# Pooled attention, then four attention experts: two batches' first output with tokens on the rows, turned by the DMA crossbar

## The chip, the core and the metric

The kernel runs on one core of a Trainium2 chip. The core has a matrix engine (PE, with a separate row for its weight loads, PEld), a vector engine (DVE), a scalar engine (ACT), a general engine (POOL) and a queue for transfers (SP). Data live in SBUF, 128 partitions; PE writes only to PSUM, which has eight banks of 512 fp32 columns in each partition, and DVE and ACT read it from there. The metric is the device time of one execution in microseconds (us); lower is better.

## What is computed

Eight batches of 576 tokens with eight heads of 64. Keys and values are averaged over groups of 8 tokens (72 pooled keys), each token attends to them, and the output, heads side by side, is the input x (576 x 512) of a mixture of four causal attention experts, of which each token takes the two with the largest gate.

```python
k_p = k.reshape(B, H, Sp, pool, D).mean(axis=3)
v_p = v.reshape(B, H, Sp, pool, D).mean(axis=3)
attn = softmax(scale * np.matmul(q, k_p.transpose(0, 1, 3, 2)))
x = np.matmul(attn, v_p).transpose(0, 2, 1, 3).reshape(B, S, H * D)
...
for e in range(E):
    q, k, v = x @ wq[e], x @ wk[e], x @ wv[e]
    a = softmax(causal(scale * (q @ k.transpose(0, 2, 1))))
    ye = a @ v @ wo[e]
    out += (gate weight of expert e) * ye
```

## The kernel before

The program is one long list of steps, the string SEQ, written out by a planner. Each token of it names a step, its arguments, its batch, the PSUM bank or banks it uses, and, with a trailing d, that a copy goes to DVE and not to ACT. The list is walked once; every engine gets its own instructions in that order and works them off strictly in that order. So the list sets the order of work on PE, ACT, DVE, POOL and SP, and the PSUM banks. Capital letters are PE's steps, small letters what reads their banks.

The steps of one batch b, with the lines that the profile shows:

- L loads q, k and v, converted to bf16 on the way, on POOL's queue (L124). Three buffers of each kind are used in turn.
- PK, PV pool keys and values on PE (L205, as most matmuls); kc, kt and vc bring the results to SBUF (kpT; vp, 96 pooled rows by 8 heads by 64). u turns q by 32 x 32 blocks on DVE (L281).
- E, e: scores of the 8 heads, pooled keys on the rows, tokens in the columns; ACT takes the exponential (L314) into eta.
- D, d, x: the sum over the pooled keys, by matmuls of eta with a constant matrix (onesd), for 4 heads at a time, each in a strip of 32 rows; ACT takes its logarithm (d, L333) and then exp of its negative (x, L337), which leaves the reciprocal in rza.
- O, o: vp times eta, again in four strips of 32 rows, so that a head's features lie on the rows and the tokens in the columns; DVE multiplies by rza (o, L360 for the 512 main tokens, L351 for the last 64) into xT, which is x turned, features on the rows.
- P, p: xT times the experts' query and key weights; p copies to qk. V, v: xT as weights, times the experts' value and gate weights; v copies values (vaug) and gate logits. g: the gates, ten small steps.
- S, s: causal score blocks; s is the exponential on ACT (L477, L471), a the causal mask on POOL (L494, L486).
- B, bz, bg, b: scores times values with a column of ones that gives the sum; reciprocal, gate factor and multiplication on DVE (L529, L531, L536) into osc, tokens on the rows.
- T, t turn osc on PE and copy it into oT (L214, L196); in batches 2 to 5, F does that by the DMA crossbar from SP's queue instead (L561 for the last 64 tokens, L564 for the 512 others).
- Y, y, z: oT times the output weights, the copy to ofin (L196) and the store (L599, L595 for the last 64 tokens of two batches), from SP's queue.

Batches go in pairs: batches 2n and 2n + 1 share one xT, in which the last 64 tokens of both lie in one block of 128 columns. Before, xT is laid out as 128 partitions x 4 feature groups x 1152 columns. The steps of neighbouring batches are interleaved, so that while ACT takes exponentials of one batch, PE works on another. A wait arises where a step of one engine needs a result, or a bank, of another that is not there yet; all later steps of that engine stand behind it. At the start, H steps are matmuls on zeros that fill PE's idle time.

Of the kernel before, what the change touches and what calls it, by code (L numbers as in the profile page):

```python
# [21 lines left out]
def kernel(  # L22
# [33 lines left out]
    KR = 96  # L56
# [70 lines left out]
    def plain(c):  # L127
        return xTs[1][0:KR].rearrange("p f n -> p (f n)").bitcast(FP32)[:, 512 * c : 512 * c + 512]
# [94 lines left out]
    def mcols(b):  # L223
        return slice(640 * (b % 2), 640 * (b % 2) + MAIN)

    def tcols(b):
        return slice(MAIN + 64 * (b % 2), MAIN + 64 * (b % 2) + TAIL)


# [41 lines left out]
    def vc(b, bank, dve):  # L271
        copy(dve, vps[b % 2][:], psum[0:KR, bank, :].rearrange("j (h d) -> j h d", d=D))
# [67 lines left out]
    def Ov(b, bank, g, t):  # L340
        got = pieces(b, g)
        for j, cols, o in got:
            for u in range(2) if g == 2 else [t]:
                for i, h, eta in heads(b, j, cols):
                    at_ = o * 2 + TAIL * u if g == 2 else o
                    mm(psum[32 * i : 32 * i + 32, bank, at_ : at_ + eta.shape[1]], vps[b % 2][:, h, u::2], eta)

    def ov(b, bank, dve, g, t):
        xT, rz = xt(b), part(rzas[b % 2], b, g)
        if g == 2:  # L350
            nc.vector.tensor_tensor(  # L351
                out=xT[:, :, tcols(b)].rearrange("p (g t) n -> p g t n", t=2),
# [4 lines left out]
        else:  # L357
            got = pieces(b, g)
            m = mcols(b).start
            nc.vector.tensor_tensor(  # L360
                out=xT[:, 2 * got[0][0] + t : 2 * got[-1][0] + t + 1 : 2, m + got[0][1].start : m + got[0][1].stop],
                in0=psum[:, bank, :].rearrange("p (g n) -> p g n", g=len(got)), in1=rz, op=MULT,
            )
# [69 lines left out]
    def P(b, bank, nm, ep):  # L433
        jobs = [(m, e) for m in "qk" for e in range(NEP)] if nm == "t" else [(nm, ep)]
        cols, n = (tcols(b), TAIL) if nm == "t" else (mcols(b), MAIN)
# [122 lines left out]
    def crossbar(b, ep, tail):  # L558
        oT, own = oTs[2 * (b // 2 % 2) + ep], osc(b, ep)
        if tail:  # L560
            nc.sync.dma_start(out=oT[:, tcols(b)], in_=own[half(b), 4 * (1 - b % 2), :], transpose=True)  # L561
        else:
            c = b % 2
            nc.sync.dma_start(out=oT[:, mcols(b)].rearrange("p (c n) -> p c n", n=128), in_=own[:, c : c + 4, :].rearrange("p c n -> p (c n)"), transpose=True)  # L564
# [26 lines left out]
    def z(b, c, queue):  # L591
# [9 lines left out]
    MATRIX = {"PK": PK, "PV": PV, "E": Es, "D": Dn, "O": Ov, "V": V, "P": P,  # L601
# [7 lines left out]
        H1:0@0 W1:0 PK1:0@0 L_k0:1 E0:0@24 kc1:0 H1:0@1 L_k1:1 kt1:0d H1:0@1 e00:0 H1:0@0 H1:0@0 H1:0@0 u1:0 L_k2:1  # L609
        e01:0 L_q0:1 E2:0@02 E1:0@46 e20:0 e21:0 L_q1:1 e11:0 D2:0@2 D0:0@3 d0:0 PV:0@0 L_q2:1 e10:0 H1:0@1 H1:0@1  # L610
        vc:0d H1:0@1 H1:0@1 x0:0 O01:0@3 c0:0d L_q3:1 O10:0@4 d2:0 D1:0@5 o01:0 x2:0 O00:0@0 O20:0@2 d1:0 O11:0@1 o00:0
        H1:0@6 H1:0@3 x1:0 H1:0@3 W2:0 c2:0d H1:0@3 c1:0d H1:0@0 H1:0@0 o10:0 H1:0@0 H1:0@0 W3:0 o11:0 H1:0@0 H1:0@0
        o20:0 P_q0:0@3 c3:0d L_v0:1 P_k0:0@2 p_q0:0 L_v1:1 P_t0:0@1 p_k0:0 L_v2:1 PK:1@3 p_t0:0 S00:0@4 L_k0:2 kc:1
        S03:0@0 S01:0@6 P_k1:0@2 s03:0 kt:1d s01:0 L_k1:2 P_q1:0@3 u1:1 L_k2:2 p_k1:0 s00:0 u0:1 a01:0 E1:1@06 a03:0
        p_q1:0d L_q0:2 e10:1 c4:0d E2:1@24 L_q1:2 e20:1 e21:1 L_q2:2 E0:1@02 e11:1 V2:0@4 a00:0 L_q3:2 e00:1 V3:0@5
        v2:0d V1:0@6 v3:0d e01:1 V0:0@4 L_v0:2 v1:0d D0:1@5 v0:0d D2:1@7 PV:1@0 d0:1 g1:0 D1:1@6 L_v1:2 H1:0@1 g0:0
        vc:1d x0:1 H1:0@1 H1:0@1 g2:0 d1:1 O01:1@0 L_v2:2 g3:0 O11:1@1 d2:1 O00:1@5 o01:1 x2:1 O20:1@6 O10:1@7 x1:1
        S02:0@2 o00:1 W4:0 H1:0@4 s02:0 o11:1 S10:0@4 L_k0:3 o20:1 S11:0@0 s10:0 o10:1 S12:0@2 L_k1:3 PK:2@6 g4:0 s11:0
        V2:1@7 L_k2:3 kc:2 P_t0:1@4 s12:0 kt:2d V0:1@6 L_q0:3 P_q0:1@5 u0:2 a02:0 p_t0:1 v0:1 u1:2 v2:1 E0:2@02 L_q1:3
        p_q0:1 g5:0 B01:0@4 g6:0 e00:2 L_q2:3 g7:0 P_k0:1@5 g8:0 g9:0 a10:0 bz01:0 e01:2 bg01:0 E1:2@06 L_q3:3 b01:0  # L620
        p_k0:1d B00:0@4 a11:0 e10:2 V3:1@2 L_v0:3 bz00:0 bg00:0 B10:0@5 b00:0 PV:2@3 e11:2 a12:0 bz10:0 v3:1d D0:2@4
        P_k1:1@0 vc:2d L_v1:3 d0:2 bg10:0 b10:0 E2:2@26 x0:2 L_v2:3 O00:2@4 p_k1:1d e21:2 D1:2@5 O01:2@1 e20:2 o00:2
        O10:2@6 L_k0:4 d1:2 O11:2@0 o01:2 PK:3@7 x1:2 L_k1:4 S01:1@2 kc:3 S02:1@4 P_q1:1@1 s01:1 o10:2 L_k2:4 o11:2
        s02:1 V4:1@7 L_q0:4 T01:0@6 p_q1:1d S00:1@2 t01:0 L_q1:4 v4:1d S03:1@4 s00:1 S11:1@0 P_q1:2@6 u1:3 a02:1 s03:1
# [129 lines left out]
```

## Time and profile before

| | us |
|---|---|
| median of three runs | 157.75 |
| lowest and highest | 156.88, 159.96 |
| the profiled execution, own time | 156.05 |
| its span, first to last instruction | 154.3 |

The time of an execution holds a little more than the span. The busy shares of the engines, the table of windows and the groups by line are shown in the prediction, each where it is used. A group's row reads: line, engine, operation, written tile <- read tiles, partitions x elements and type, count | busy us in total, mean ns of one | idle us of the engine before them, and what ended it. A row of the timeline reads: start us, length us, engine, line, operation, count of merged instructions.

The inputs are loaded throughout the first part: the last of POOL's load instructions starts at 85.1 us, and the first crossbar transfer of SP's queue at 91.8 us.

### The profile page before, as it was taken

Reading aid. Unit: us, or ns where it says so; the run is one execution under the profiler, and the core shown is the slowest. Engines: PE = TensorE matmul, PEld = TensorE weight load, DVE = VectorE, ACT = ScalarE, POOL = GpSimd, SP = SyncE. Lnnn points to the kernel's source line nnn. Section 1 sums busy time; section 2 is a strip of 40 time slices with the busy share of each in tenths; the row PEclk is TensorE's granted clock in tenths of the full one; section 3 lists DMA queues with packets and bytes.
Section 4 is the critical chain, followed back from the end, with each engine's and each line's share of the span. In section 5 each row is a group of like instructions: output and inputs, shape, how many; then the busy total and the mean of one; then the engine's idle time right before and its main releaser. Section 6 shows DMA issues by size and latency. Waiting matters only on the chain.

```text
span 154.3 us, 5462 instructions
## 1 busy us (share of the span) xinstructions
PE 145.2 (94%) x2137; PEld 79.0 (51%) x2137; DVE 126.5 (82%) x405; ACT 135.5 (88%) x254; POOL 89.3 (58%) x161
## 2 busy tenths in 40 slices
PE   6986998999999999999999999999999999999970
PEld 2431452546464567346645674455454676556730
DVE  1652958699998999999999999989989988979860
ACT  4328749999999999999999999999999999989970
POOL 6986578978898989785899333133300254424300
PEclk9999999999999999999999999999999999999999
DMA  5999999999999999999999992273501652287894
GB/s 117 141 175 180 181 179 179 180 181 187 181 179 178 179 180 182 195 225 222 180 179 183 210 144 47 38 248 132 174 4 68 167 154 43 49 314 247 328 372 132
DMA packets 68602, 26.38 MB, mean 171 GB/s; under 512 B 62688, under 2 KB 63712, under 8 KB 68576
## 3 DMA queue, kind: packets, MB, share of 16 engines
q0 software_dynamic: 57408, 15.02, 97.6%
q1 hardware_dynamic: 10944, 10.62, 21.8%
q8 instruction: 16, 0.26, 0.7%
q10 hardware_dynamic: 224, 0.39, 0.7%
q14 instruction: 10, 0.08, 0.2%
HBM read 30.42 MB, written 9.44 MB: 258 GB/s over the span
## 4 chain that ended last, share of the span: by engine, by line
PE 65%; DMA 19%; DVE 6%; POOL 3%; issue 2%; ACT 1%; DVEq 0%; POOLq 0%
PE psum L205 63%; DMA qraw<-in_q_dram 14%; DMA wst_q<-in_moe_wq_dram 5%; PE psum L214 1%; DVE qT L281 1%; POOL qraw L124 1%; DVE xT L360 1%; POOL kraw L124 1%; DVE qk L196 1%; POOL etb L494 1%; ACT eta L314 1%; PE psum L193 0%; DVE osc L536 0%; DVE kpT L196 0%; DVE ofin L196 0%
## 5 line engine op out<-in xcount | busy, mean ns | idle before, releaser
L477 ACT ACTIVATE etb<-psum 128x1024 bf16<-128x1024 f32 x48 | 47.2, 1031 | 0.8 <-PE psum L205 0.2
L494 POOL TENSOR_SCALAR_AFFINE_SELECT etb<-etb 128x256 bf16<-128x256 bf16 x64 | 25.5, 410 | 28.7 <-ACT etb L477 28.4
L314 ACT ACTIVATE eta<-psum 96x1024 bf16<-96x1024 f32 (+1 forms) x48 | 36.0, 811 | 4.8 <-PE psum L205 4.4
L124 POOL DMA_DIRECT2D qraw<-in_q_dram x30 | 19.6, 655 | 3.6 <-DMA vraw<-in_v_dram 1.5
L124 POOL DMA_DIRECT2D kraw<-in_k_dram x25 | 19.0, 762 | 3.9 <-PE psum L205 2.1
L360 DVE TENSOR_TENSOR xT<-psum,rza 128x512 bf16<-128x512 f32 x32 | 20.2, 678 | 1.2 <-PE psum L205 0.9
L205 PE MATMUL psum<-wvg,xT 128*128 128x260 bf16 x144 | 21.1, 275 | 0.0
L205 PEld LDWEIGHTS <-etb 128*128 128x128 bf16 x480 | 17.9, 97 | 6.3 <-issue 3.2
L124 POOL DMA_DIRECT2D vraw<-in_v_dram x24 | 18.4, 772 | 4.2 <-PE psum L205 3.2
L205 PE MATMUL psum<-vaug,etb 128*128 128x65 bf16 x480 | 20.1, 193 | 0.0
L205 PE MATMUL psum<-wop,oT 128*128 128x512 bf16 (+1 forms) x74 | 19.6, 374 | 0.2 <-DVE oT L196 0.2
L205 PE MATMUL psum<-xT,wkp 128*128 128x512 bf16 (+1 forms) x128 | 19.6, 286 | 0.1
L205 PE MATMUL psum<-xT,wqp 128*128 128x512 bf16 (+1 forms) x128 | 19.6, 286 | 0.0
L536 DVE TENSOR_TENSOR osc<-psum,gt 128x256 bf16<-128x256 f32 (+2 forms) x40 | 16.8, 422 | 1.1
L205 PE MATMUL psum<-qk 64*128 64x64 bf16 (+4 forms) x192 | 15.9, 277 | 0.2 <-DVE xT L360 0.2
L205 PEld LDWEIGHTS <-xT 128*128 128x128 bf16 x144 | 12.2, 97 | 6.4 <-issue 3.5
L281 DVE STREAM_TRANSPOSE qT<-qraw 128x576 f32<-128x576 f32 x16 | 12.9, 824 | 3.0 <-DMA qraw<-in_q_dram 3.0
L205 PE MATMUL psum<-qT,kpT 32*128 32x64 bf16 (+1 forms) x256 | 13.2, 289 | 1.7 <-DVE qT L281 0.9
L196 DVE CAST qk<-psum 128x512 bf16<-128x512 f32 (+1 forms) x22 | 14.2, 644 | 0.6 <-PE psum L205 0.2
L193 PE MATMUL psum<-warm 128*128 128x512 bf16 x47 | 12.8, 418 | 1.3 <-DVE onesd L163 1.3
L196 DVE COPY ofin<-psum 128x512 f32<-128x512 f32 (+1 forms) x17 | 11.0, 668 | 2.1 <-PE psum L205 1.8
L337 ACT ACTIVATE rza<-rza 128x512 f32<-128x512 f32 (+1 forms) x24 | 12.4, 528 | 0.3
(76 smaller groups left out, 218.1 us busy)
## 6 DMA issues: line engine op xcount, KB each, us to landing
out_dram<-ofin SPq DMA_DIRECT2D x31, 256.0 KB, 2.5
vraw<-in_v_dram POOLq DMA_DIRECT2D x24, 192.0 KB, 7.1
kraw<-in_k_dram POOLq DMA_DIRECT2D x21, 192.0 KB, 7.5
qraw<-in_q_dram POOLq DMA_DIRECT2D x28, 144.0 KB, 7.7
out_dram<-ofin SPq DMA_DIRECT2D x7, 128.0 KB, 3.1
qraw<-in_q_dram POOLq DMA_DIRECT2D x2, 288.0 KB, 6.1
xT<-in_k_dram SPq DMA_DIRECT2D x2, 192.0 KB, 2.8
kraw<-in_k_dram POOLq DMA_DIRECT2D x4, 96.0 KB, 5.3
```

Of the source, the lines that this page charges most:

```text
L124: nc.gpsimd.dma_start(out=dst, in_=src)
L193: nc.tensor.matmul(out=psum[rows, bank, :], lhsT=warm[:, rows], rhs=warm[:], start=True, stop=True)
L196: (nc.vector.tensor_copy if dve else nc.scalar.copy)(out=out, in_=in_)
L205: nc.tensor.matmul(out=out, lhsT=lhsT, rhs=rhs, start=start, stop=stop)
L214: nc.tensor.transpose(out=out[s], in_=in_[:, s], identity=ident[0:n, 0:n])
L281: nc.vector.transpose(out=dst.rearrange("p (a s n) -> p a n s", s=32, n=n), in_=src.rearrange("p (a n d) -> p a n d", n=n, d=32))
L314: nc.scalar.activation(out=dst, in_=src, func=EXP, scale=ATT_EXP_SCALE)
L337: nc.scalar.activation(out=rz, in_=rz, func=EXP, scale=-1.0)
L360: nc.vector.tensor_tensor(out=xT[:, 2 * got[0][0] + t : 2 * got[-1][0] + t + 1 : 2, m + got[0][1].start : m + got[0][1].stop], in0=psum[:, ...
L477: nc.scalar.activation(out=et[:, ep, :, eo : eo + n], in_=psum[:, bank : bank + 2, 0:n], func=EXP, scale=MOE_EXP_SCALE,)
L494: nc.gpsimd.affine_select(out=blk, in_=blk, pattern=[[0, 2], [1, 128]], compare_op=ISGE, fill=0.0, base=0, channel_multiplier=-1,)
L536: nc.vector.tensor_tensor(out=osc(b, ep)[:, own, :].rearrange("p c (e d) -> p e c d", e=2), in0=o[:, :, :, 0:HD], in1=gt.to_broadcast([128 ...
```

## The change

In batches 6 and 7, steps D, d, x, O and o are replaced. A new step N multiplies, for a block of 128 tokens (five blocks a batch, the last one with 64 tokens of use), eta as the weights with vp as the moving operand, head by head: the output has tokens on the rows and, in two neighbouring banks, 8 heads of 65 columns, the 65th of which is the sum. For that, vp gets a 65th column with the constant of onesd, and eta a padding of 64 columns. nz takes the reciprocal of the 8 sums on DVE, n multiplies and writes xn, 128 tokens x 512 features. G (turn_x) moves xn to xT by the DMA crossbar on SP's queue, three transfers a batch: two with two blocks each and one with the last 64 tokens. xn shares its memory with rza.

xT is laid out anew for all batches, 128 partitions x 9 blocks x 4 feature groups x 128 tokens, and the order of a head's features in vp and of the feature groups is adapted (rows_of), so that o, P and V read and write other addresses in all batches. The list SEQ is new from its third line on, including the banks and which copies go to DVE; the order of the load instructions among themselves stays. In its steps, 24 d and 24 x become 18 each, 40 o become 30, and 10 N, 10 nz, 10 n and 6 G come.

```diff
-    vps = bufs(2, [KR, H, D], BF16, "vp")
+    vps = bufs(2, [KR, H, D + 1], BF16, "vp")
...
-    etas = bufs(2, [KR, H, S], BF16, "eta")
-    rzas = bufs(2, [128, 2, S], FP32, "rza")
-    xTs = bufs(2, [128, NFC, PAIRW], BF16, "xT")
+    etaws = bufs(2, [KR, H * S + TAIL], BF16, "eta")
+    etas = [t[:, 0 : H * S].rearrange("k (h s) -> k h s", h=H) for t in etaws]
+    xns = bufs(2, [128, NTC, DM], BF16, "xn")
+    rzas = [t[:].rearrange("p c n -> p (c n)").bitcast(FP32)[:, 0 : 2 * S].rearrange("p (g s) -> p g s", g=2) for t in xns]
+    rzns = bufs(2, [128, H], FP32, "rzn")
+    xTs = bufs(2, [128, NPC, NFC, 128], BF16, "xT")
...
+        for t in vps:
+            nc.vector.memset(t[:, :, D : D + 1], 0.0)
+            for c in range(3):
+                nc.vector.memset(t[32 * c : 32 * c + 24, :, D : D + 1], DSC)
+        for t in etaws:
+            nc.vector.memset(t[:, H * S :], 0.0)
...
+    def rows_of(fc):
+        return 2 * (fc % 2) + fc // 2
+
+    def mains(b):
+        return slice(5 * (b % 2), 5 * (b % 2) + 4)
...
-        copy(dve, vps[b % 2][:], psum[0:KR, bank, :].rearrange("j (h d) -> j h d", d=D))
+        copy(dve, vps[b % 2][:, :, 0:D].rearrange("j h (t r) -> j h t r", t=2),
+             psum[0:KR, bank, :].rearrange("j (h r t) -> j h t r", r=32, t=2))
...
-                out=xT[:, 2 * got[0][0] + t : 2 * got[-1][0] + t + 1 : 2, m + got[0][1].start : m + got[0][1].stop],
-                in0=psum[:, bank, :].rearrange("p (g n) -> p g n", g=len(got)), in1=rz, op=MULT,
+                out=xT[:, m + cols.start // 128 : m + cols.stop // 128, 2 * t + got[0][0] : 2 * t + got[-1][0] + 1, :]
+                .rearrange("p c g n -> p g c n"),
+                in0=psum[:, bank, :].rearrange("p (g c n) -> p g c n", g=len(got), n=128),
+                in1=rz.rearrange("p g (c n) -> p g c n", n=128), op=MULT,
...
+    def nat(bank):
+        return psum[:, bank : bank + 2, :].rearrange("p g (i n) -> p (g i) n", n=128)
+
+    def Nx(b, bank, c):
+        c0 = 128 * c if c < 4 else MAIN - 64 * (b % 2)
+        for h in range(H):
+            mm(nat(bank)[:, h, 0 : D + 1], etaws[b % 2][:, S * h + c0 : S * h + c0 + 128], vps[b % 2][:, h, :])
+
+    def nx(b, bank, step, c):
+        rows = slice(0, 128) if c < 4 else half(b)
+        o, rz = nat(bank)[rows], rzns[c % 2][rows]
+        if step == "nz":
+            nc.vector.reciprocal(out=rz, in_=o[:, :, D])
+        else:
+            nc.vector.tensor_tensor(
+                out=xns[b % 2][rows, c].rearrange("p (t h r) -> p h t r", t=2, h=H),
+                in0=o[:, :, 0:D].rearrange("p h (t r) -> p h t r", t=2),
+                in1=rz.unsqueeze(2).unsqueeze(3).to_broadcast([rz.shape[0], H, 2, 32]), op=MULT,
+            )
+
+    def turn_x(b, k):
+        xn, o = xns[b % 2], b % 2
+        if k == 2:
+            nc.sync.dma_start(out=xt(b)[:, 4, :, half(b)], in_=xn[half(b), 4, :], transpose=True)
+        else:
+            m = mains(b).start + 2 * k
+            nc.sync.dma_start(out=xt(b)[:, m : m + 2].rearrange("p c f n -> p (c f) n"),
+                              in_=xn[:, 2 * k : 2 * k + 2].rearrange("p c n -> p (c n)"), transpose=True)
...
-            wide(psum[:, bank, 0:VG], xt(b)[:, fc, 128 * place(b, c) : 128 * place(b, c) + 128], wvg[:, fc, :],
+            wide(psum[:, bank, 0:VG], xt(b)[:, place(b, c), rows_of(fc), :], wvg[:, fc, :],
...
-                wide(psum[:, bank, n * j : n * j + n], wqk[m, e][:, fc, :], xt(b)[:, fc, cols],
+                wide(psum[:, bank, n * j : n * j + n], wqk[m, e][:, fc, :], xt(b)[:, places, rows_of(fc), cols],
```

The steps N, nz, n and G of batch 6 in the new list, up to the first reader of the main tokens:

```diff
+        S10:4@0 e21:6 vc:7 S01:4@2 g1:4 N0:6@4 F00:2 s10:4 g2:4 B00:3@6 nz0:6 n0:6 P_k1:5@7 s01:4 a10:4 bz00:3 bg00:3
+        N2:6@0 b00:3 N1:6@4 p_k1:5 a01:4 V1:5@2 nz2:6 F01:3 n2:6 N3:6@6 Y2:1@3 v1:5 nz1:6 n1:6 V3:5@0 y2:1p Y1:1@2
+        nz3:6 v3:5 G0:6 n3:6 P_t0:5@1 zs2:1 y1:1p S11:4@4 p_t0:5d S12:4@6 zs1:1 S02:4@2 s11:4 g3:4 B01:3@1 g4:4 g5:4
+        G1:6 g6:4 V2:5@0 s12:4 bz01:3 a11:4 Y4:1@4 bg01:3 b01:3 P_q1:5@5 v2:5 y4:1dp a12:4 s02:4 E2:7@06 g7:4 F00:3
+        zs4:1 B10:3@4 g8:4 g9:4 e20:7 p_q1:5d a02:4 e21:7 S00:4@2 g0:5 S01:5@0 bz10:3 S00:5@6 bg10:3 s00:4 P_k0:6@5
...
```

More of the change, by code (lines that the diff above doesn't have):

```diff
@@ L345, in Ov @@
                     at_ = o * 2 + TAIL * u if g == 2 else o
-                    mm(psum[32 * i : 32 * i + 32, bank, at_ : at_ + eta.shape[1]], vps[b % 2][:, h, u::2], eta)
+                    mm(psum[32 * i : 32 * i + 32, bank, at_ : at_ + eta.shape[1]], vps[b % 2][:, h, 32 * u : 32 * u + 32], eta)
     def ov(b, bank, dve, g, t):
@@ L351, in ov @@
             nc.vector.tensor_tensor(
[L352 removed]
+                out=xT[:, 4, :, half(b)].rearrange("p (t g) n -> p g t n", t=2),
                 in0=psum[:, bank, 0 : 4 * TAIL].rearrange("p (g t n) -> p g t n", g=2, t=2),
@@ L613 @@
[L613 to L617, printed above, removed]
@@ new lines @@
+        H1:0@0 e00:0 H1:0@0 L_q0:1 E1:0@02 E2:0@46 H1:0@0c e11:0 H1:0@0c L_q1:1 H1:0@0c e20:0 e21:0 PV:0@2 L_q2:1 e10:0
+        D2:0@3 D0:0@6 vc:0d H1:0@4 H1:0@4 d2:0 d0:0 c0:0d O20:0@7 L_q3:1 O01:0@2 c1:0d x0:0 D1:0@3 O11:0@6 O00:0@0 d1:0
+        O10:0@1 o01:0 H1:0@4 H1:0@4 x1:0 W2:0 H1:0@3 o00:0 H1:0@3 x2:0 H1:0@2 o10:0 H1:0@2 H1:0@0 W3:0 H1:0@0 o11:0
+        H1:0@0 H1:0@0 c3:0d P_q0:0@6 c2:0d L_v0:1 o20:0 P_k0:0@7 p_q0:0 L_v1:1 P_t0:0@1 p_k0:0 L_v2:1 PK:1@6 p_t0:0
+        S00:0@2 L_k0:2 kc:1 S02:0@0 S03:0@4 s00:0 P_k1:0@7 kt:1d L_k1:2 s03:0 P_q1:0@6 u1:1 s02:0 L_k2:2 u0:1 a00:0
@@ new lines @@
+        S11:1@4 a02:1 s12:1 T10:0@7 P_q1:2@6 u1:3 L_q2:4 s03:1 t10:0d S10:1@2 s11:1 L_q3:4 p_q1:2d S00:1@0 V1:1@7 kt:3d
+        a12:1 s00:1 V3:2@6 v1:1d P_q0:2@4 L_v0:4 v3:2d s10:1 g1:1 E0:3@06 L_v1:4 p_q0:2d x2:2 g0:1 B11:0@5 e00:3 a01:1
+        g2:1 P_k0:2@4 L_v2:4 bz11:0 bg11:0 e01:3 b11:0 E1:3@02 a03:1 p_k0:2d L_k0:5 V0:2@5 e11:3 g3:1 T11:0@4 g4:1
+        L_k1:5 PK:4@6 v0:2d PV:3@7 e10:3 L_k2:5 kc:4 D1:3@5 O20:2@2 P_k1:2@3 vc:3d t11:0 L_q0:5 d1:3 o20:2 kt:4 g5:1
+        E2:3@06 L_q1:5 g6:1 B02:0@2 p_k1:2 g7:1 P_t0:2@5 g8:1 e20:3 a11:1 g9:1 u1:4 e21:3 B12:0@3 L_q2:5 p_t0:2 S00:2@0
```

138 lines of the change are left out of this document (65 added, 73 removed).

## The prediction

> **What bounds the kernel now.** I read the page first, its busy line and its chain of waits.
>
> ```profile
> PE 145.2 (94%) x2137; PEld 79.0 (51%) x2137; DVE 126.5 (82%) x405; ACT 135.5 (88%) x254; POOL 89.3 (58%) x161
> ```
> ```profile
> PE 65%; DMA 19%; DVE 6%; POOL 3%; issue 2%; ACT 1%; DVEq 0%; POOLq 0%
> ```
>
> Shares over the whole span mix the start, where the engines wait for the first loads, with the rest. So the second view is the table of windows, over the stretch from 28 us, when the first batch is through, to 149 us, when only the last output rows are left.
>
> ```profile
> core 0 of [0], span 154.3 us
> core 0: us, PE busy (x) PEld busy (x) DVE busy (x) ACT busy (x) POOL busy (x), PEclk, DMA share, GB/s
> 28.00:149.00 121.00, 120.61 (x1856) 68.67 (x1854) 110.61 (x362) 118.33 (x226) 67.54 (x127) 1.00 1.16 171
> ```
>
> In these 121.00 us ACT works 118.33 and PE shows 120.61: two engines without room, and DVE has 121.00 - 110.61 = 10.4 us of room. The chain names PE, but it follows one predecessor at each step, and on an engine that never pauses that is its own previous instruction; it would have run along ACT just as well. The clock is 1.00 throughout. The Trainium skill ("Perfetto Trace Analysis", Identifying the Most-Contended Engine) holds that matmul busy time says little about PE's headroom, since matmuls overlap, and that the busy share of the weight loads is the better sign; here that is 68.67 of 121.00, 57%. What follows from this is the second rival.
>
> So a saving counts in full where it comes off ACT as long as PE can follow, and DVE's costs nothing while its 10.4 us last.
>
> **ACT.** For batches 6 and 7 the logarithm and the exponential of the reciprocals go: D, d and x disappear, 6 ACT instructions a batch. The groups by line, kept apart by form, for ACT:
>
> ```profile
> L196 ACT COPY ofin<-psum 128x512 f32<-128x512 f32 x19 | 11.1, 600 | 0.4 <-PE psum L205 0.4
> L337 ACT ACTIVATE rza<-rza 128x512 f32<-128x512 f32 x16 | 10.0, 632 | 0.2
> L333 ACT ACTIVATE rza<-psum 128x512 f32<-128x512 f32 x16 | 9.3, 596 | 0.3
> ...
> L196 ACT CAST vaug<-psum 128x256 bf16<-128x256 f32 x13 | 5.0, 395 | 0.0
> ...
> L196 ACT COPY L<-psum 128x4 f32<-128x4 f32 x13 | 2.5, 196 | 0.0
> L337 ACT ACTIVATE rza<-rza 128x128 f32<-128x128 f32 x8 | 2.5, 318 | 0.1
> L333 ACT ACTIVATE rza<-psum 128x128 f32<-128x128 f32 x8 | 2.2, 276 | 0.0
> ...
> L196 ACT CAST vp<-psum 96x512 bf16<-96x512 f32 x1 | 0.6, 582 | 0.0
> ```
>
> Each batch has two of 0.596, two of 0.632, one of 0.276 and one of 0.318: 3.05 us, so 6.1 us for the two. The new orders give part of it back, for they hand copies from DVE to ACT: counted in both orders, ACT gets 5 more y (0.600 each), 3 more vc (0.582), 3 more v (0.395 + 0.196) and 1 more P_t copy (an estimate: as vaug, 0.395), and loses 5 two-column-block t (128x256, as vaug, 0.395) and 2 kt (as vp, 0.582). That is 3.00 + 1.75 + 1.77 + 0.40 - 1.98 - 1.16 = 3.8 us. Net: -2.3 us of durations. Successive ACT instructions overlap a little (in the x19 row, 19 x 0.600 = 11.4 against 11.1 busy), so I count **-2.0 us**.
>
> **DVE.** The multiplications o go (four of 128x512 and one of 128x256 a batch), and five pairs of a reciprocal nz and a multiplication n come.
>
> ```profile
> L360 DVE TENSOR_TENSOR xT<-psum,rza 128x512 bf16<-128x512 f32 x32 | 20.2, 678 | 1.2 <-PE psum L205 0.9 <-ACT rza L333 0.4
> ...
> L196 DVE COPY ofin<-psum 128x512 f32<-128x512 f32 x16 | 10.6, 683 | 1.5 <-PE psum L205 1.2 <-ACT qk L196 0.2
> L536 DVE TENSOR_TENSOR osc<-psum,gt 128x256 bf16<-128x256 f32 x24 | 10.2, 424 | 0.7
> L196 DVE CAST vaug<-psum 128x256 bf16<-128x256 f32 x23 | 9.6, 418 | 2.2 <-PE psum L205 2.2
> L196 DVE CAST vp<-psum 96x512 bf16<-96x512 f32 x7 | 4.7, 677 | 2.9 <-PE psum L205 2.7 <-ACT rza L333 0.2
> ...
> L536 DVE TENSOR_TENSOR osc<-psum,gt 128x384 bf16<-128x384 f32 x8 | 4.4, 554 | 0.2
> L529 DVE RECIPROCAL rzb<-psum 128x4 f32<-128x4 f32 x24 | 4.0, 174 | 1.0 <-PE psum L205 0.4
> ...
> L196 DVE COPY L<-psum 128x4 f32<-128x4 f32 x23 | 3.4, 150 | 0.0
> L351 DVE TENSOR_TENSOR xT<-psum,rza 128x256 bf16<-128x256 f32 x8 | 3.2, 406 | 0.0
> ```
>
> The n is new in form (PSUM read in runs of 64, factor broadcast), but osc has that form: 424 ns at 256 columns and 554 at 384, 130 for 128 more, so 684 at 512, beside 678 for the o it replaces. The reciprocal of 8 columns I take as that of 4, 0.174. Per batch: 5 x (0.684 + 0.174) - 4 x 0.678 - 0.406 = +1.2 us, +2.4 for two. The copies handed to ACT take off 5 x 0.683 + 3 x 0.677 + 3 x 0.568 + 0.418 = 7.6, and the t and kt that come back cost at most 5 x 0.418 + 2 x 0.554 = 3.2. Net about -2 us, on the engine with room: **0** in the sum. The other layouts of xT and vp change addresses within these same writes, and the rows of memsets come at the start, before the first k is pooled; both at nothing, at most 10 memsets of the size of a reciprocal of 4 columns at the worst, 1.7 us.
>
> **PE.** Out go, per batch, D (4 + 4 + 8 matmuls) and O (16 + 16), 48 in all; in come 40 of 96 rows, 128 weight columns and 65 columns. PE's timeline around batch 7's O (columns: start, length, then the group):
>
> ```profile
> 113.75 0.71 PE L205 MATMUL psum<-vaug,etb 128*128 128x65 bf16 x18
> 114.30 0.59 PE L205 MATMUL psum<-wop,oT 128*128 128x512 bf16 x2
> 114.83 0.30 PE L205 MATMUL psum<-qT,kpT 32*128 32x64 bf16 x16
> 115.06 0.40 PE L205 MATMUL psum<-eta,onesd 96*32 96x512 bf16 x4
> 115.39 1.04 PE L205 MATMUL psum<-xT,wqp 128*128 128x512 bf16 x4
> 116.36 0.52 PE L205 MATMUL psum<-eta,onesd 96*32 96x512 bf16 x20
> 116.70 1.27 PE L205 MATMUL psum<-eta,vp 96*32 96x512 bf16 x48
> 117.90 0.39 PE L205 MATMUL psum<-wop,oT 128*128 128x512 bf16 x1
> ```
>
> Matmuls overlap, so I price from start to start. 116.36 to 117.90 (1.54) holds batch 7's D and O except D1, and besides 24 small ones of batch 6; D1 is 115.06 to 115.39 (0.33), the small ones by the kpT row 0.23 / 16 = 14 ns each, 0.34. So 1.53 us go per batch. An N matmul has the 65 columns and the 128 weight columns of vaug's: (114.30 - 113.75) / 18 = 31 ns, 40 make 1.22. Bounds: 14 ns by the kpT row and 82 ns by the D1 row (0.33 / 4), so for both batches between -1.9 and +3.5; I take 31 ns, the nearest row, **-0.6 us**. V's weights stay pieces of 128. P now streams its 512 columns in four pieces, which no row shows: between nothing and, if each of three new pieces cost as much as a small matmul, 3 x 14 ns in 16 matmuls of 8 batches, 5.4 us. I take nothing, since no column is added and all lie in the same partitions; the other end belongs to case E below.
>
> **Queues.** N needs two free neighbouring banks where D and O needed one; N, then nz, n and G, stand between the exponentials of batch 6 and P and V. G is a crossbar transfer on SP's queue, three a batch, twice as wide as the crossbar transfers there are (two chunks of 512 columns).
>
> ```profile
> L564 SPq DMA_TRANSPOSE oT<-osc x8: 1212/1236/2502, 93.2 to 133.6; - x8
> ```
> ```profile
> DMA to landing us min/median/max: 2.2/2.5/4.4
> ```
>
> SP issues one in 1.24 us (at most 2.50) and it lands after 2.5 (4.4). In the new order SP has two stores of batch 1's output ahead of G1 of batch 6, and whoever waits for those stores' copies holds G1. Behind n3:6 the new PE order has, ahead of P_k0:6, P_q1:5 (0.97 by the wqp row), Y4:1 (0.53), E2:7 (0.23) and 30 vaug matmuls (0.93), 2.7 us, and besides a P_t, a V and six score groups: about 4.5 to 5 us by my estimate. The median transfer is hidden, so is what hangs on it; a 4.4 us one behind a slow issue is not. Six more issues are 7.4 us on SP, which has nothing else then but stores and the other transfers: 0. The Trainium skill ("VectorE: DVE Perf Modes", Rules for kernel authors) would turn a full 128x128 block on TensorE if PSUM is an acceptable destination and use the crossbar otherwise; what its being right would mean here is the fourth case.
>
> **The sum.** Against the profiled execution, 156.05 us with its span of 154.3: ACT -2.0, PE -0.6, DVE and queues 0. If both engines are full, the smaller saving alone would count at places where PE is late and the larger where ACT is; I take a point between, -1.5, and so 154.55. The runs shown lie higher (median 157.75, 156.88 to 159.96), so I carry the -1.5 over to the median: **156.2 us**.
>
> **The rivals.** *PE was never full (B).* Then ACT's whole 2.0 us come back. The tail adds to it: behind batch 7's last exponential (s03:7) ACT has 15 instructions now and 11 in the new order; four t of 0.395 fewer, 1.6 us. 157.75 - 3.6 = 154.2. For it: 57% of weight-load time, and ACT's 118.33. Against: copies moved onto ACT sit elsewhere than the removed work. By the skill's rule on weight-load time this is the case. *Banks (C).* If each N at the head of PE's queue waits for the last reader of its second bank, that costs one DVE pass, 0.68, with V, P, S and B queued behind it, and ACT starves for S. From the third of the ten N on the gain of 1.5 is used up; with eight, 8 x 0.68 - 1.5 = +3.9, **161.7, slower than before**. For it: PE and ACT run with no slack that could absorb it. Against: DVE's room, and batches 0 to 5 ask for up to four banks at once for E. *Crossbar exposed (D).* Issue 2.50 and landing 4.4 against some 4.7 hidden: 2.2 late, at four places (G0/G1 and G2 of two batches) 8.8; less 1.5, 165. *A redrawn order eats the gain (E).* The whole list of steps is new from its third line on: 157.8.
>
> **Chances.** Forecast 0.45 (own range 155.0 to 157.5), B 0.25, C 0.14, D 0.05, E 0.11. Two per cent, about what a measurement of this kernel tells from no change, is 3.2 us: faster is below 154.6, slower above 160.9. B is over that line some seven times in ten and the forecast's lower edge one time in ten: 0.17 + 0.04 = 0.21. Slower: two thirds of C, all of D and a little of E: 0.17. Same: 0.62. The range leaves out the lower third of B and the upper half of C with D: 153.4 to 160.5.
>
> **What would show it.** In the new profile: rza groups at 12 + 6 instead of 16 + 8 each; PE's N between two starts at about 0.25 us for 8; n near 0.68; G landing in 2.5 to 3; no wait of PE on xT before P_k0:6, P_t0:6, V0:7, P_t0:7. Against me: PE or the weight loads waiting for DVE ahead of N (C), a wait on a transfer into xT (D), or ACT idle over 4 us between 28 us and the end of the exponentials (E or C).

## The result, and the profile after

| | median us | runs | lowest, highest |
|---|---|---|---|
| before, beside it | 157.31 | 4 | 155.96, 159.96 |
| after | 158.84 | 4 | 158.59, 159.88 |

The ratio is 1.0123, with a 95% interval of 1.0083 to 1.0163: slower by less than two per cent, and no change lies outside the interval. (It leaves disturbed runs out, so it is not the quotient of the two medians.) The forecast was 156.2. The profiled execution of after is its slowest, 159.88 us with a span of 158.1; the spans of the three others are 156.9 to 157.2, so its waits may be longer than theirs. The profile of before (156.05 us), by contrast, is one of its fastest executions.

The page's busy line and its chain of waits, after:

```profile
PE 146.5 (93%) x2121; PEld 80.3 (51%) x2121; DVE 125.2 (79%) x417; ACT 133.3 (84%) x250; POOL 89.4 (57%) x161
...
PE 58%; DMA 21%; ACT 8%; DVE 7%; issue 2%; POOL 1%; DVEq 0%; POOLq 0%
```

ACT's busy time fell by 135.5 - 133.3 = 2.2 us, close to the forecast, and DVE's by 1.3. Neither is in the time. The windows show where it went. First the stretch of the forecast, 28 to 149 us, of after; then the sums of 100 to 130 us, where batches 6 and 7 go through the new steps, of before and of after:

```profile
28.00:149.00 121.00, 117.51 (x1795) 67.21 (x1793) 106.31 (x348) 113.86 (x216) 68.72 (x128) 1.00 1.24 170
```
```profile
sum 30.00, PE 30.00 PEld 17.39 DVE 26.71 ACT 29.45 POOL 7.63; mean PE 10.00 PEld 5.80 DVE 8.90 ACT 9.82 POOL 2.54
```
```profile
sum 30.00, PE 27.58 PEld 16.59 DVE 24.02 ACT 24.33 POOL 7.10; mean PE 9.19 PEld 5.53 DVE 8.01 ACT 8.11 POOL 2.37
```

Before, both engines are full there (30.00 and 29.45 of 30). After, PE stands still for 2.4 us and ACT for 5.7, more than twice the relief it was given. PE's waits behind 100 us name what it stood for (engine, line, what ended it: us in total, times, longest):

```profile
PE psum L214 <- DMA xT<-xn: 2.4, 2, 1.3
PE psum L214 <- DVE oT L205: 0.3, 1, 0.3
PE psum L214 <- DMA oT<-osc: 0.3, 1, 0.3
```

Two waits for the crossbar transfers of xn into xT, one in each batch; none for DVE ahead of N, so no bank was missing. The pieces of the chain (start, length) and SP's own timeline show how the first of them comes about:

```profile
103.67 0.70 DVE xn L393
104.42 2.30 PE psum L214 x30
106.71 3.32 DMA xT<-xn
110.17 9.42 PE psum L214 x94
...
123.19 4.51 DMA xT<-xn
127.74 7.46 PE psum L214 x119
```
```profile
103.36 2.15 SPq L405 DMA_TRANSPOSE xT<-xn  x1
105.60 1.01 SPq L642 DMA_DIRECT2D out_dram<-ofin  x2
106.71 1.29 SPq L405 DMA_TRANSPOSE xT<-xn  x1
```

The multiplication n3 of batch 6 is done at 103.67 + 0.70 = 104.37, but its transfer (G1) is issued only at 106.71: SP is still issuing the one before it (2.15 us) and then two stores of batch 1. 2.3 us in the queue and 3.3 for the transfer make 5.7 us from n3 to PE's next reader. What PE had meanwhile ends here:

```profile
108.06 0.82 PE L214 MATMUL psum<-qk 64*128 64x512 bf16 x8
110.17 1.02 PE L214 MATMUL psum<-xT,wkp 128*128 128x512 bf16 x4 [1.28 <-DMA xT<-xn]
```

That is at 108.88, 4.5 us behind n3. In batch 7, n3 ends at 121.72 + 0.69 = 122.41 and G1 is issued 0.8 us later, at 123.19. It lands only after 4.51, and PE has run out at 126.65, 4.2 us behind n3:

```profile
121.72 0.69 DVE L393 TENSOR_TENSOR xn<-psum,rzn 128x512 bf16<-128x512 f32 x1
126.06 0.59 PE L214 MATMUL psum<-wop,oT 128*128 128x512 bf16 x2
127.74 1.04 PE L214 MATMUL psum<-xT,wkp 128*128 128x512 bf16 x4 [1.08 <-DMA xT<-xn]
```

So the waits are 1.28 and 1.08 us. The slow issue at the first place and the late landing at the second both stand beside a fetch of PE's instructions; the last section shows this.

The rest of what the forecast priced came out as it said. The new multiplication n, the logarithms and exponentials that are left (x12, x12; the tile is called xn now, since both share their memory), and two starts of PE around one N:

```profile
L349 ACT ACTIVATE xn<-xn 128x512 f32<-128x512 f32 x12 | 7.7, 641 | 0.2
L345 ACT ACTIVATE xn<-psum 128x512 f32<-128x512 f32 x12 | 7.2, 604 | 0.0
L393 DVE TENSOR_TENSOR xn<-psum,rzn 128x512 bf16<-128x512 f32 x8 | 5.5, 691 | 0.3
```
```profile
99.26 0.43 PE L214 MATMUL psum<-vp,eta 96*128 96x65 bf16 x8
99.53 0.65 PE L214 MATMUL psum<-vaug,etb 128*128 128x65 bf16 x16
```

n takes 691 ns (684 forecast), the eight matmuls of an N 0.27 us (0.25 forecast).

### The profile page after: what moved, and what is told of

Read it like the earlier page. It is cut to its first block, busy times and chain, and to the rows that moved or that the text cites. A ratio compares the mean times of both kernels' runs of the same rounds, so it can differ in the third digit from the quotient of the medians.

```text
span 158.1 us, 5450 instructions
## 1 busy us (share of the span) xinstructions
PE 146.5 (93%) x2121; PEld 80.3 (51%) x2121; DVE 125.2 (79%) x417; ACT 133.3 (84%) x250; POOL 89.4 (57%) x161
## 4 chain that ended last, share of the span: by engine, by line
PE 58%; DMA 21%; ACT 8%; DVE 7%; issue 2%; POOL 1%; DVEq 0%; POOLq 0%
PE psum L214 57%; DMA qraw<-in_q_dram 9%; DMA xT<-xn 5%; DMA wst_q<-in_moe_wq_dram 5%; ACT eta L326 3%; DVE xn L393 3%; ACT etb L520 2%; DMA oT<-osc 2%; PE psum L223 2%; DVE rzn L391 1%; DVE xT L372 1%; ACT xn L349 1%; ACT xn L345 1%; POOL kraw L127 1%; DVE qT L293 0%
## 5 line engine op out<-in xcount | busy, mean ns | idle before, releaser
L214 PE MATMUL psum<-wop,oT 128*128 128x512 bf16 (+1 forms) x74 | 21.1, 374 | 0.7 <-DVE oT L205 0.3
L214 PE MATMUL psum<-wvg,xT 128*128 128x260 bf16 x144 | 20.6, 275 | 0.0
L372 DVE TENSOR_TENSOR xT<-psum,xn 128x512 bf16<-128x512 f32 x24 | 15.1, 680 | 0.8 <-ACT xn L349 0.5
L205 ACT COPY ofin<-psum 128x512 f32<-128x512 f32 (+1 forms) x25 | 14.2, 588 | 1.8 <-PE psum L214 1.5
L202 PE MATMUL psum<-warm 128*128 128x512 bf16 (+1 forms) x47 | 13.9, 443 | 1.3 <-DVE onesd L166 1.3
L214 PE MATMUL psum<-qT,kpT 32*128 32x64 bf16 (+1 forms) x256 | 12.7, 289 | 2.1 <-DVE qT L293 1.5
L205 ACT CAST qk<-psum 128x512 bf16<-128x512 f32 (+1 forms) x19 | 9.9, 525 | 3.9 <-PE psum L214 3.9
```

What stands on the lines that cost most here:

```text
L202: nc.tensor.matmul(out=psum[rows, bank, :], lhsT=warm[:, rows], rhs=warm[:], start=True, stop=True)
L205: (nc.vector.tensor_copy if dve else nc.scalar.copy)(out=out, in_=in_)
L214: nc.tensor.matmul(out=out, lhsT=lhsT, rhs=rhs, start=start, stop=stop)
L372: nc.vector.tensor_tensor(out=xT[:, m + cols.start // 128 : m + cols.stop // 128, 2 * t + got[0][0] : 2 * t + got[-1][0] + 1, :] .rearrang ...
```

## The experiments

All are timed beside the kernel before on the same chip; its medians there were 157.21 (runs 1 to 4), 156.87 (5 to 8), 157.07 (9 to 11) and 157.45 (12).

**1. The layouts alone.** The changed code, with the list of the kernel before: D, d, x, O and o in all batches, but xT, vp, eta and the memsets laid out anew.

```diff
-    SEQ = the list of after
+    SEQ = the list of before
```

> The changed code with the old list of steps: batches 6 and 7 go by D, d, x, O and o again, while the new layouts of xT and vp, the memsets and the padding stay. Theory one (the crossbar transfers of G hold PE up, 1.44 us ahead of P_k0:6 and 1.25 ahead of P_k0:7): nothing of that is here, so it runs as the kernel before, 157.3 within 0.6. Rival, the layouts cost (P in pieces of 128 columns, changed writes of o and vc): slower than before by 1 us or more, up to the 5.4 of the dear end.

157.54, ratio 0.9977 (0.9930 to 1.0024). P's reads in four pieces, o's writes in runs of 128 and the memsets cost nothing. The loss lies in the new list or the new steps.

**2. The transfers ahead of the stores.** G1 of batches 6 and 7 stands directly behind its n3 in the list.

```diff
-        nz3:6 v3:5 G0:6 n3:6 P_t0:5@1 zs2:1 y1:1p S11:4@4
+        nz3:6 v3:5 G0:6 n3:6 G1:6 P_t0:5@1 zs2:1 y1:1p S11:4@4
...
-        nz3:7 n3:7 S03:5@4 zs4:3
+        nz3:7 n3:7 G1:7 S03:5@4 zs4:3
```

> The changed kernel, but the second wide transfer G1 of batch 6 and of batch 7 is issued ahead of the stores that stood before it on SP's queue (two stores each). Theory one, in the form that SP's queue is what makes the transfer late: G1:6 issues some 1.1 us earlier and G1:7 some 0.8, and G1:7 no longer lands behind two stores (4.5 us), so most of the 2.7 us of waiting goes: 156.4 to 157.3. In the form that the transfer itself is too long for the cover: the waits shrink by less than half, 158 to 158.8. Rival, the order or the banks cost the time: 158.8, unchanged.

157.98, ratio 1.0056 (1.0017 to 1.0095). PE's waits for transfers behind 100 us, and the landing of the transfers:

```profile
PE psum L214 <- DMA xT<-xn: 0.7, 1, 0.7
PE psum L214 <- DMA oT<-osc: 0.5, 1, 0.5
```
```profile
DMA to landing us min/median/max: 3.1/3.4/4.9
```

Batch 6's wait is gone, batch 7's is 0.7. About half of the loss goes with the place in SP's queue. The two intervals overlap, but the ratios differ by 0.0067, with some 0.0056 on either side (the two half-widths, 0.0040 and 0.0039, as the root of the sum of their squares).

**3. The transfers of batches 6 and 7 aside.** G writes to q buffers that nobody reads any more; P and V of these batches take older data from xT, so their turned output is left out of the result.

```diff
-            nc.sync.dma_start(out=xt(b)[:, m : m + 2].rearrange("p c f n -> p (c f) n"),
+            nc.sync.dma_start(out=aside[:, 1024 * k : 1024 * k + 1024].rearrange("p (g n) -> p g n", n=128),
```

> The changed kernel, but G writes into the q buffers that are no longer needed, and P and V of batches 6 and 7 read what batches 2 and 3 left in xT: this leaves the turned output of batches 6 and 7 out of the result, every instruction runs, and nobody waits for a G. Theory one: both waits (2.7 us in the profile) are gone, 155.8 to 156.5. Rival, order or banks: 158 or more, with PE held up elsewhere.

159.30, ratio 1.0118 (1.0070 to 1.0167): the expectation of 155.8 to 156.5 missed. PE arrived earlier and met the next transfer of the same queue, one of the second attention's output (waits, then PE's timeline, then the window):

```profile
PE psum L214 <- DMA oT<-osc: 2.2, 1, 2.2
```
```profile
132.38 0.60 PE L214 MATMUL psum<-vaug,etb 128*128 128x65 bf16 x14
135.17 0.39 PE L214 MATMUL psum<-wop,oT 128*128 128x512 bf16 x1 [2.18 <-DMA oT<-osc]
135.71 1.91 PE L214 MATMUL psum<-xT,wqp 128*128 128x512 bf16 x4 [0.15 <-issue]
```
```profile
130.00:140.00 10.00, 7.66 (x100) 4.97 (x101) 5.36 (x23) 6.29 (x13) 2.71 (x7) 0.83 0.55 86
```

That transfer took 4.1 us to land, and behind PE's gap the granted clock fell: four matmuls took 1.91 us that take 1.02 in the row of after above. Taking one transfer off the path shows nothing as long as another stands behind it.

**4. The new list with the old steps.** In the list of after, N, nz, n and G of batches 6 and 7 are replaced by D, d, x, O and o at the same places.

```diff
-        S10:4@0 e21:6 vc:7 S01:4@2 g1:4 N0:6@4 F00:2 s10:4 g2:4 B00:3@6 nz0:6 n0:6 P_k1:5@7
+        S10:4@0 e21:6 vc:7 S01:4@2 g1:4 D0:6@4 D1:6@5 F00:2 s10:4 g2:4 B00:3@6 d0:6 d1:6 x0:6 x1:6 P_k1:5@7
...
```

> The new list of steps with the old work: in place of the five N of batches 6 and 7 stand D and O in the same banks, in place of nz and n stand d, x and o, and G is left out. ACT has then 6.1 us of durations more than in the changed kernel and 3.8 more than before. If ACT alone is the bound: 157.3 + 3.4 = 160.7 (durations overlap a little). If PE is as much a bound: 157.5 to 158.8. Theory one predicts no wait of PE on a transfer into xT here. If the new order itself holds PE up (the rival of a redrawn order), the waits of PE elsewhere are longer than the 1 us that the kernel before has in all.

160.13, ratio 1.0147 (1.0092 to 1.0203), between the two expectations. ACT isn't the only bound here: from 100 to 130 us it works 27.68 of 30 us and PE 27.99, and PE's longest waits there are for ACT, 1.0 and 0.6 us. The old steps don't do better in the new list; it was planned for the others, so this alone doesn't say how good the list is.

**5 and 6. All crossbar transfers aside, after and before.** Both kernels with every transfer of the crossbar written to dead buffers (in batches 2 to 5 the last projection reads old data or zeros; in after, batches 6 and 7 as in run 3), and with oT filled with zeros at the start.

```diff
+        for t in oTs:
+            nc.vector.memset(t[:], 0.0)
...
-            nc.sync.dma_start(out=oT[:, ocols(b, True)], in_=own[half(b), 4 * (1 - b % 2), :], transpose=True)
+            nc.sync.dma_start(out=oT[:, 2048 + 64 * i : 2112 + 64 * i], in_=own[half(b), 4 * (1 - b % 2), :], transpose=True)
...
```

> The changed kernel, with every transfer of the crossbar written to dead buffers: the three of batches 6 and 7 each, and those of the second attention's output of batches 2 to 5. They are issued as before and nobody waits for them; the turned outputs of these batches are left out of the result (batches 6 and 7 project old data, the last projection of batches 2 to 5 reads old data or zeros), and the four output buffers are filled with zeros once at the start. To be read against the next run, which is the kernel before with the same second half of the edit. Theory one (the change only loses because its transfers stand on TensorE's path): this run comes out below the next one, by the forecast's 1 to 2 us, at about 155. Theory two (TensorE bounds this kernel as much as ScalarE, so ScalarE's relief is worth little even with no transfer in the way): the two differ by under 0.7 us, TensorE's own 0.6 us at most.

> The kernel before, with the crossbar transfers of the second attention's output of batches 2 to 5 written to dead buffers, issued as before and with nobody waiting for them; the last projection of these batches reads old data or zeros, so that its result is left out. It is the partner of the run before. In the profile of before these transfers held TensorE for some tenths of a us, so 156.5 to 157.3 under both theories; if a transfer that lands late was worth more than that in the median run, 155.5 to 156.5.

After: 159.03, ratio 1.0130 (1.0085 to 1.0174). Before: 156.89, ratio 1.0027 (0.9990 to 1.0063). So the kernel before owes its transfers nothing that these times show, and theory one of run 5 falls. Theory two isn't met either: the two are 2.1 us apart and not under 0.7. But the run of after isn't clean. At its start PE waits 2.0 us for DVE, and the clock falls:

```profile
PE psum L204 <- DVE kf L275: 2.0, 1, 2.0
```
```profile
0.00:28.00 28.00, 24.37 (x245) 10.00 (x246) 14.77 (x51) 12.84 (x23) 19.94 (x32) 0.94 1.50 164
```

The clock of 0.94 in the first 28 us stands against 1.00 in after itself (the profile of run 6 has such a dip later, 0.95 from 28 to 60 us). How much of the time this start costs isn't shown. Run 9 repeats it without the zeros, and with the transfers of batches 2 and 3 as they were.

**7. Later readers.** Run 2, with P_k0 of batch 7 behind S10 of batch 6, and Y4 of batch 5 behind B11 of batch 6.

```diff
-        P_k0:7@0 a12:6 y2:2dp S11:5@4 F11:4 a02:5 p_k0:7d zs2:2 S10:6@2
+        a12:6 y2:2dp S11:5@4 F11:4 a02:5 zs2:2 S10:6@2 P_k0:7@0 p_k0:7d
...
-        Y4:5@3 a02:6 bz00:6 g0:7 B11:6@4
+        a02:6 bz00:6 g0:7 B11:6@4 Y4:5@3
```

> The run with the two transfers ahead of the stores, and besides the order of TensorE changed at two places: the first projection of batch 7 that reads a turned chunk goes behind a score step of batch 6 (about 1 us later), and a last projection of batch 5 goes behind an output step of batch 6. Theory one (what is left of the loss stands at those two waits, 0.7 and 0.5 us in the profile of that run): 0.5 to 1 us less than its 157.98, so 157.0 to 157.5, the kernel before. Theory two (the waits are only where an order that is less tight shows, and the gap moves on): 157.8 to 158.3.

157.75, ratio 1.0080 (1.0043 to 1.0118): theory two. The profile has a new wait in place of the two.

```profile
PE psum L214 <- DVE m L450: 1.5, 1, 1.5
```

The profile puts it down to DVE, but the weight load of the same product waits for a transfer:

```profile
PEld L214 <- DMA oT<-osc: 1.7, 1, 1.7
```

It is F00 of batch 4, which lands at 134.95; PE goes on at 135.00. Run 3 ran into the same transfer. So the gap moved on to another transfer, which landed late (4.35 us).

**8. PE's instruction fetches moved.** Run 2, with ten of the H matmuls of the start replaced by eight times as many small ones.

```diff
-        H1:0@4
+        R8:0@4
...
+            elif name == "R":
+                for _ in range(*a):
+                    mm(psum[:, int(bank), 0:64], warm[:, 0:128], warm[:, 0:64])
```

> The run with the two transfers ahead of the stores, with ten filler multiplications of 512 columns in the first 20 us replaced by eight of 64 columns each: the same columns, 70 instructions more. It moves the points at which TensorE fetches its next 256 instructions by 70 instructions, some 2 to 4 us earlier in the part behind 100 us. Theory one (a transfer lands 1.5 to 2 us late where such a fetch falls into its flight): the transfer of batch 7 that landed in 4.86 us lands in 3 to 3.5, since the fetch no longer falls into it, and another one of SyncE's transfers that is now in flight at a fetch lands late; the time moves by up to 1 us in either direction. Theory two (it is late because of where its data or its queue stand): it lands in 4.5 to 5 us again, and the time stays at 158.

158.10, ratio 1.0102 (1.0059 to 1.0144). The transfer of batch 7 landed in 3.11 us and not 4.86, and others became late (section on the hardware, below). PE's wait of 0.7 us for it is gone from the profile, and no wait for a transfer into xT is left there. The time is no better for it.

**9. No wait for a transfer, without the zeros.** After, with G aside as in run 3 and, in batches 4 and 5 only, the second attention's transfers aside as well (their last projection reads older data; the turned outputs of these four batches are left out).

```diff
+        main, rest = oT[:, ocols(b, False)], oT[:, ocols(b, True)]
+        if b > 3:
+            i, raw = 2 * (b % 2) + ep, qraws[2][:].rearrange("p g a t d -> p (g a t d)")
+            main, rest = raw[:, 512 * i : 512 * i + 512], raw[:, 2048 + 64 * i : 2112 + 64 * i]
```

> The changed kernel, with the crossbar transfers of batches 6 and 7 and those of the second attention's output of batches 4 and 5 written to dead buffers (issued as before, nobody waits for them; the turned outputs of these four batches are left out of the result, older data of the same buffers are read instead), and without the zero fill at the start that the earlier run of this kind had. The kernel before gains nothing from the like (ratio 1.0027). Theory one (the transfers are the whole loss; the earlier run's 1.013 came from its zero fill and a lower clock at the start): a ratio of 0.997 to 1.002. Theory two (the new order loses some 0.5 us ahead of 100 us as well, which TensorE's 0.3 to 0.6 us just pay for): 1.001 to 1.006. Theory three (the order behind 100 us is itself worse, transfers or not): 1.008 to 1.015, and lost time of TensorE behind 100 us in the profile well above the 3.2 us of the kernel before.

158.12, ratio 1.0049 (1.0009 to 1.0089): theory two. The waits behind 100 us, all of them, and the sum of 100 to 130 us:

```profile
PE psum L214 <- DVE oT L205: 0.3, 1, 0.3
PE psum L223 <- DVE osc L579: 0.3, 1, 0.3
```
```profile
sum 30.00, PE 29.67 PEld 18.34 DVE 26.36 ACT 26.75 POOL 7.97; mean PE 9.89 PEld 6.11 DVE 8.79 ACT 8.92 POOL 2.66
```

With no crossbar transfer in the way PE is full again (29.67 of 30), and ACT works 26.75 where it worked 29.45 before. So ACT's 2.7 us of relief stand there as idle time: PE sets the pace. And the kernel is still no faster than before.

**10. ScalarE busy again.** Run 2, with four additional exponentials, two in each batch.

```diff
+            elif name == "X":
+                nc.scalar.activation(out=warm[:], in_=warm[:], func=EXP)
```

> The run with the two transfers ahead of the stores (157.98 there, a ratio of 1.0056), with four additional exponentials of 128x512 on ScalarE, two in each of batches 6 and 7 at the place where the matrix products with tokens on the rows are read; nobody reads their result. At about 0.6 us each they give ScalarE 2.4 us back, more than the 2.0 us that the change took from it. Theory one (TensorE is the bound behind 100 us, and ScalarE now idles there): 0 to 0.6 us more, a ratio of 1.005 to 1.010. Theory two (ScalarE's relief is in the time, and hides part of the loss): 1.5 to 2.4 us more, a ratio of 1.015 to 1.021.

158.40, ratio 1.0111 (1.0055 to 1.0167), between the two theories. 100 to 130 us, run 2 and then run 10:

```profile
sum 30.00, PE 28.98 PEld 17.85 DVE 25.51 ACT 25.83 POOL 7.64; mean PE 9.66 PEld 5.95 DVE 8.50 ACT 8.61 POOL 2.55
```
```profile
sum 30.00, PE 29.02 PEld 18.06 DVE 25.74 ACT 27.43 POOL 7.71; mean PE 9.67 PEld 6.02 DVE 8.58 ACT 9.14 POOL 2.57
```

In the profile ACT takes 1.6 us more there and PE does as much as without it; the span grew by 0.3 (155.9 to 156.2). The times say 0.0055 of 157 us, 0.9 us, with an interval of 1.1 on either side. ACT's time counts for little or for a part, not in full; more can't be told.

**11 and 12. Towards a better one.** Run 11 is run 8 with Y3 of batch 4 behind P_q1 of batch 7. Run 12 is run 2 with this move, the move of Y4 of run 7, and O20 of batch 1, which waits 0.5 us for ACT in the new list, behind PK of batch 2.

```diff
-        O20:1@0 O10:1@7 s01:0 PK:2@1
+        O10:1@7 s01:0 PK:2@1 O20:1@0
...
-        Y3:4@0 s01:7 bz11:5 F00:5 a11:6 P_q1:7@4
+        s01:7 bz11:5 F00:5 a11:6 P_q1:7@4 Y3:4@0
```

> The run with the instruction fetches moved (two transfers ahead of the stores, ten fillers replaced; 158.1 there) and one last projection of batch 4, which waited 0.57 us there for its transfer of the second attention's output, put behind the query projection that follows it (0.9 us later). Nothing of the computation is left out. Theory one (the waits for transfers are what is left): no wait for a transfer in the profile, 0.4 to 0.7 us less than 158.1 beside the same kernel before, a ratio of 1.003 to 1.007. Theory two (the order ahead of 100 us and the tail hold the rest): the wait goes and the ratio stays at 1.008 to 1.011.

> The run with the two transfers ahead of the stores (157.98, a ratio of 1.0056), with three instructions of TensorE put later in the new order and nothing left out: a tail product of batch 1, which waits 0.5 us for ScalarE to empty its bank in every run with the new order (at 33 us), behind the key pooling that follows; and two last projections, of batches 4 and 5, each behind the product that follows it, of which one waited 0.5 us for its crossbar transfer. Theory one (what is left of the loss is such single waits, whether a transfer or a bank ends them): the waits at 33 us and at the last projection of batch 5 go, and 0.5 to 1 us of the time with them, a ratio of 0.999 to 1.003. Theory two (TensorE makes the gap a few instructions later, since ScalarE or VectorE is what it then meets): 0 to 0.3 us less, a ratio of 1.004 to 1.007.

158.68, ratio 1.0079 (1.0040 to 1.0119), with no wait for a crossbar transfer left in its profile; and 158.24, ratio 1.0057 (1.0019 to 1.0096). Theory two both times. PE's waits from 28 to 100 us, run 2 and then run 12:

```profile
PE psum L214 <- ACT etb L520: 0.5, 1, 0.5
PE psum L214 <- ACT eta L326: 0.2, 1, 0.2
```
```profile
PE psum L214 <- DVE xT L372: 0.6, 1, 0.6
PE psum L214 <- POOL etb L537: 0.5, 1, 0.5
```

The wait of 0.5 us for ACT, at 33.5 us, is gone. In its place stands one of 0.6 us for DVE, at 33.4, and another of 0.5 us follows at 40.8. No version beat the kernel before.

To see the whole of it I added up PE's lost time. For each step of PE I took the time from its start to the next one's, and as its nominal time the value below which 30% of the steps of that kind lie over all the profiles; what is above it is lost. (The traces of runs 2 and 9 lack 16 records of matmuls, and were aligned by the operands.)

```
                 nominal   lost 0-60   60-100   100-end   PE's end
before            132.5       9.7        3.3       3.1      149.82
after             132.1      10.2        3.9       6.5      154.04
run 2             132.1      10.2        3.3       5.0      151.82
run 9             132.1      10.4        3.9       3.5      151.10
run 12            132.1      10.3        3.6       4.8      152.02
```

(To the sum of a row come the 1.3 us before PE's first step.) The new steps take 0.4 us from PE. With the transfers on its path it loses 6.5 - 3.5 = 3.0 us more behind 100 us, in this slowest profile of after, and run 9, with none there, still 0.4 us more than before. Ahead of 100 us, in batches whose steps are the old ones, the rows of the new list lose 0.5 to 0.7 us more up to 60 us and up to 0.6 from there on. But a row is one execution, and that of before is one of its fastest. Summed in the same way, the profiles of runs 7 and 8, which have the new list too, lose no more than before ahead of 60 us (9.3 and 9.7). So the table doesn't show that the list costs anything there.

## Why the prediction was wrong

**The step that failed is the one on the queues**: "The median transfer is hidden, so is what hangs on it", with a 0 for the queues in the sum. Its cover was about right, 4.5 us measured at the first place against an estimated 4.5 to 5 (4.2 at the second). What it had to cover was priced too low. It put in the transfer's own landing, 2.5 us, from rows of transfers half as wide; the double-wide ones landed in 3.0 to 4.5. It named the two stores ahead of G1 but gave them no price, and priced a slow issue in case D alone: together the slow issue and the stores held G1 for 2.3 us. 2.3 + 3.3 is more than the cover at the first place, 0.8 + 4.51 at the second. It also had no term for the fetches of PE's instructions, beside which both late pieces stand (last section). Case D, crossbar exposed, was the right mechanism at the wrong size (four places of 2.2 us, where there were two, of 1.3 and 1.1), with a chance of 0.05. Its size added the issue to a landing that already counts from the start of the issue, and its 4.4 us come from the narrower transfers of L561, since the landing line that is shown is that of all transfers into oT; L564 alone has 3.6 at most. Moving the transfers ahead of the stores brought the ratio from 1.0123 to 1.0056. With no wait for a crossbar transfer left it was 1.0049 in run 9 and 1.0079 in run 11, so these waits hold a part of the loss, and how large a part the intervals leave open.

**The second fault is "I take a point between, -1.5".** ACT's -2.0 was right as a duration and counted for nothing that could be shown: run 9 has 2.7 us less work on ACT while PE is full. Run 10 leaves room for a part of it. The most that the steps could bring was PE's part, forecast as -0.6 and by the table 0.4. Between two full engines the smaller saving is the most that can count, not a mean of the two. By the Trainium skill's rule on weight-load time ("Perfetto Trace Analysis", Identifying the Most-Contended Engine) PE would have had headroom at 57%, which was case B, 154.2 (the same section asks for the share of peak matmul work beside it, which wasn't worked out here). Run 9, where PE's steps fill the time with weight loads at 61% and a relieved ACT brings nothing, speaks against it for this kernel.

**Case E, the redrawn order eats the gain,** is what is left by exclusion: run 1 rules the layouts out, and run 9 the waits for transfers as all of it. Without any wait for a crossbar transfer the kernel was 0.1 to 0.9% slower than before in run 9, and 0.4 to 1.2% in run 11, which leaves nothing out. Runs 7 and 12 removed single waits and saw others in their place, and run 11 removed one with no gain that can be told, so no single step that was moved holds it. Which property of the list does stays open, and so does whether it is the list alone: a list of the old order ahead of 100 us with the new steps behind it wasn't tried.

**Right were** N (0.27 us, no wait for banks: case C fell), n, DVE at nothing, and P's four pieces at nothing (run 1). Of the signs named against the forecast, two came: a wait on a transfer into xT, and ACT idle for over 4 us. The starting point was off as well: 157.75 was the median of three runs, and larger samples gave 156.87 to 157.45.

## What to carry to other kernels

A transfer on the path costs its wait in the issuing queue and its landing, which these views count from the start of its issue: take both from rows, at the width it will have, and read the queue's order around it before calling it hidden. Where two engines are full, relieving one is worth at most what the other saves. And when a planner redraws the whole list for one local edit, price the new list as a change of its own, since in a kernel without slack a removed wait can show up again further on, as in runs 3, 7 and 12.

## What the runs showed of the hardware

PE's instructions arrive as transfers too: in each profile the trace has 16 packets of 16 KB on a queue of the kind "instruction" (q8), one for every 256 of PE's instructions, matmuls and weight loads together (2 x 2121 in after; runs 8 and 11, with 2 x 70 more, have 17), each taking 0.9 to 1.8 us. The trace's records of SP's transfers beside them:

```
transfer     run      issued   landed   us     a fetch starts
G1:7         after    123.19   127.69   4.51   124.54
G1:7         run 2    120.43   125.29   4.86   123.29
G1:7         run 8    120.98   124.09   3.11   none between (120.06, 127.85)
F00:4        run 3    131.01   135.12   4.11   132.72
F00:4        run 7    130.60   134.95   4.35   132.48
F00:4        after    132.57   135.04   2.47   134.91, 0.13 ahead of the landing
F00:3        run 8    107.08   111.61   4.53   108.97
F00:3        run 2    107.39   110.13   2.75   none between (103.16, 115.51)
```

In these rows a transfer with a fetch that starts 1.3 to 2.9 us behind its issue lands 1.4 to 1.9 us later than the same one without; a fetch that starts just ahead of the landing leaves it as it is. Run 8 moved the fetches and the delay moved with them, from G1 of batch 7 to F00 of batch 3, as expected. The landing comes in 16 parts. In run 2, where the fetch starts 2.86 us behind the issue of G1 of batch 7, 15 of them are there after 3.29 us and one alone after 4.86; in after, where it starts 1.35 us behind, the first comes after 4.36.

The issue itself is slower too. Behind 93 us, the 14 profiles have 20 crossbar issues of over 1.9 us on SP, and a fetch starts within 0.7 us of the start of every one; the 217 issues with no fetch near (from 1 us ahead to 0.75 behind) take 1.10 to 1.35 us. G0 of batch 6 takes 2.15 us in after, with a fetch at 103.88, and 1.24 in run 8, with none. By an estimate from these rows, 0.9 us for that issue and 1.4 for the landing of G1 of batch 7, the two waits of 1.28 and 1.08 us would have been 0.4 and nothing without the two fetches. Why a fetch holds up the transfers beside it, the trace doesn't show.

The clock: in run 3, half the granted clock follows a gap of PE of 2.18 us, from 135.50 to 138.92 us (0.83 over 130 to 140). Three other profiles have such a stretch near the start: 28.36 to 31.77 in run 1, 10.43 to 13.84 in run 5 and 28.94 to 32.35 in run 6. Each lasts 3.41 us, and in the 3.41 us ahead of each PE stands idle for 2.2 us (run 3), 1.6 (run 1), 2.0 (run 5) and 1.2 (run 6). The length of a single gap doesn't decide it: one of 1.22 us in run 1 comes ahead of such a stretch, those of 1.28 and 1.08 in after and of 1.53 in run 7 don't. The Trainium skill ("TensorE: Matmul & The Clock Gate", Part 1) has the clock halved after an idle window of about 3.4 us; here none of the gaps was that long.
